# Chunked attention and a squared-ReLU feed-forward on one core: the next block's attention moves to the front of the input stage

## The chip, the cores and the metric

The kernel runs on one core of a Trainium2 chip. The metric is the device time of one execution in microseconds (us); before the change its median over 7 runs is 294.36 us (292.05 to 300.25). One execution was profiled. TensorE (PE; PEld is its weight load) does the matmuls, VectorE (DVE) and ScalarE (ACT) the element-wise work, GpSimd (POOL) casts and stores, and SyncE (SP) issues the loads and the transposing DMAs.

## The reference

Attention within chunks of 64 tokens, for 8 batches, 8 heads, 576 tokens and a head size of 64, and then a feed-forward network over the 4608 tokens, with 2048 inner features:

```python
scores = scale * np.matmul(q_c, k_c.transpose(0, 1, 2, 4, 3))   # q_c, k_c, v_c: (B, H, 9, 64, 64)
scores = scores - np.max(scores, axis=-1, keepdims=True)
attn = np.exp(scores)
attn = attn / (np.sum(attn, axis=-1, keepdims=True) + 1e-09)
out = np.matmul(attn, v_c)
x = out.transpose(0, 2, 1, 3).reshape(B * S, H * D)             # (4608, 512)
h = np.maximum(x @ w_in, 0.0)                                   # w_in (512, 2048)
return (h * h) @ w_out                                          # w_out (2048, 512)
```

Inputs and output are float32; the kernel multiplies in bfloat16 and accumulates in float32.

## The kernel before

**Groups and blocks.** The tokens are cut into 18 groups of 256, and two groups make a block of 512: blocks 0 to 8, where block 1 takes group 3 before group 2. A block has an input stage (`ffn_in`, x times w_in, ReLU and square) and an output stage (times w_out). While TensorE works on one block's feed-forward, the attention of the next block's groups (`nxt`) is put between its matmuls, and the loads, casts and transposes of the block after that (`far`) run on the other engines.

**Slots.** Nothing is scheduled by a planner: every instruction is issued in the order in which the Python code reaches it (`manual_schedule`), and each engine works through its own queue in order. The order of the work is set by slots. `ffn_in` and `ffn_out` are generators; each `yield` is a slot. After each slot the loop at L570 to L579 issues one load of the block's list (if the slot is in `go_slots`) and then whatever `at(slot, f, g)` has put into the plan. In blocks 2 to 8 the input stage has 16 slots (0 to 15), one per slice of 128 inner features, and the output stage 14 (16 to 29). Block 1 takes its two groups one after the other in its input stage, so it has 32 slots there and 14 in its output stage (32 to 45). Block 0 has 16 and 16.

**The steps of a group's attention**, by the short names used in the plan:

- `C` (L209): q and k are cast to bfloat16 (`qkb`), on POOL for groups below 8 and on ACT from there on.
- `TD` (L216): one transposing DMA, issued by SP, turns `qkb` into `qkT`. Groups 0 to 3 are transposed on TensorE instead (`TE`, `TA`, `TM`, L176), with two copies of q out of PSUM on DVE and two of k on ACT (L174).
- `SC` (L224): 32 small matmuls (L234) write the scores into a PSUM tile of the pool `ps_att`, which has two buffers; ACT takes the exponential (L241) into `e`.
- `AV` (L244): two sets of 32 small matmuls (L258), each into a `ps_att` tile, then for each set a reciprocal of the row sums (L265) and a multiplication (L266) on DVE, which give `x`.
- `XT` (L272): `x` becomes `xT`, the feed-forward's input. From group 6 on this is a transposing DMA issued by SP (L279); groups 2 to 5 are transposed on TensorE (L285), and one copy takes the result out of PSUM (L290), on ACT for group 2 and on DVE for the others.

**Feed-forward.** In a slot of `ffn_in` TensorE does four matmuls (L318) into one of four `ps_ffn` banks, ACT takes the ReLU (L329), and DVE the square (L333), or ACT for three slices of a block (L331). All of them need `xT` of the whole block, except in block 1, which takes 256 tokens at a time. The output stage of block 0 is plain (L464). That of the other blocks (`ffn_out`, L351) computes the two-by-two block product with seven products instead of eight: `product` (L386) runs two slots for each of them, into two PSUM chains "n" and "m", and between them DVE forms differences of the input (`d5`, `d2`, `d1`, `d6`, `d7`: one L346 instruction of 128x2048 each, into `w_st` tiles), adds the partial results (`nm`, `n1`, `o_sb`, L346 too) and ACT copies others. The sums of quarters of w_out that the products need (`sum_quarters`) are formed on DVE in blocks 0 and 1.

**SP's queue.** The loads of q, k and v, and the transposing DMAs TD and XT, stand in one queue on SP in the order of the slots. In block 2 the loads are v of groups 6 and 7 and then q, k and v of groups 8 and 9, one in each slot; XT of groups 6 and 7 and TD of groups 8 and 9 stand among them. Each of these DMAs also waits until the one eight places ahead of it has landed. The stores go out on POOL.

The functions that the change touches, and the code that calls them:

Of the kernel before, what the change touches and what calls it, by code (L numbers as in the profile page):

```python
# [17 lines left out]
def kernel(  # L18
# [9 lines left out]
    nc = tc.nc  # L28
# [243 lines left out]
    def transpose_x(g):  # L272
        j, c = place[g]
        if j not in xTs:
            xTs[j] = att_pool.tile([128, BT // 128, n_dt, 128], BF16, name="xT", bufs=2)
        x = state.pop(("x", g))
        dst = xTs[j][:, c // 128:c // 128 + 2].rearrange("p t h q -> p (t h) q")
        if g >= FIRST_DMA_X:
            nc.sync.dma_start_transpose(out=dst, in_=x.rearrange("p t h a d -> p (t h a d)"))  # L279
            return  # L280
        ps = ps_att.tile([128, 1024], FP32, name="ps_att")
        psb = ps.bitcast(BF16)[:, 0:1024].rearrange("p (b q) -> p b q", q=128)
        for t in range(2):
            for hp in range(n_hp):
                nc.tensor.transpose(  # L285
                    out=psb[:, t * n_hp + hp, :],
                    in_=x[:, t, hp].rearrange("p a d -> p (a d)"),
                    identity=ident)
        copy = nc.scalar.copy if g == 2 else nc.vector.tensor_copy
        copy(out=dst, in_=psb)  # L290

    C, TD = cast_qk, transpose_qk_dma
# [58 lines left out]
    def ffn_out(j):  # L351

        gT = gTs.pop(j)
        HT = BT // 2
        last = j == len(blocks) - 1
        a11, a12 = gT[:, 0:HF, 0:HT], gT[:, HF:, 0:HT]  # L360
        a21, a22 = gT[:, 0:HF, HT:], gT[:, HF:, HT:]

        def difference(x, y):
            d = wst_pool.tile([128, 1024], FP32, name="w_st").bitcast(BF16).rearrange(
                "p (a f) -> p a f", a=HF)
            add(nc.vector, d, x, y, ALU.subtract)
            return d

        n_tt = HT // 128
        banks = {}  # L370

        def chain(name):
            tiles = [ps_ffn.tile([128, 512], FP32, name="ps_ffn")
                     for _ in range(n_tt if last else 1)]
            banks[name] = [(tiles[t], 0, HD, t) for t in range(n_tt)] if last else [
                (tiles[0], 0, n_tt * HD, None)]
            return [tiles[t][:, 0:HD] if last else tiles[0][:, t * HD:(t + 1) * HD]
                    for t in range(n_tt)]

        def product(name, a, b, first):  # L380
            if first:
                state["chain", name] = chain(name)
            outs = state["chain", name]
            for t in range(n_tt):
                for i in range(HF):
                    nc.tensor.matmul(  # L386
                        out=outs[t],
                        lhsT=a[:, i, t * 128:(t + 1) * 128],
                        rhs=b[:, i, :],
                        start=(first and i == 0 and (last or t == 0)), stop=(i == HF - 1),  # L390
                        skip_group_check=True)
                yield

        def parts(name):
            for tile_, lo, n, t in banks[name]:
                at_ = (t or 0) * HD
                yield tile_[:, lo:lo + n], slice(at_, at_ + n), t

        def kept(name):
            return ffn_pool.tile([128, n_tt * HD], FP32, name=name)  # L400

        def store(dma, o_sb, half, col, t):
            t0 = blocks[j][half] * GT
            if t is None:
                dma.dma_start(  # L405
                    out=out[t0:t0 + HT, col:col + HD].rearrange("(t p) d -> p t d", p=128),
                    in_=o_sb.rearrange("p (t d) -> p t d", d=HD))
            else:
                dma.dma_start(
                    out=out[t0 + t * 128:t0 + (t + 1) * 128, col:col + HD],  # L410
                    in_=o_sb[:, t * HD:(t + 1) * HD])

        def o_tile():
            return ffn_pool.tile([128, n_tt * HD], FP32, name="o_sb", bufs=4)

        d5 = difference(a11, a12)
        d2 = difference(a22, a21)
        yield from product("n", a22, b11_p_b21, True)
        n1 = kept("n1")
        for ps, cols, t in parts("n"):  # L420
            nc.scalar.copy(out=n1[:, cols], in_=ps)
        yield from product("m", a11, b12_p_b22, True)
        w = kept("nm")
        for ps, cols, t in parts("m"):
            add(nc.vector, w[:, cols], ps, n1[:, cols])
        d1 = difference(a11, a22)
        yield from product("n", d5, b22, False)
        n2 = kept("n2")
        for ps, cols, t in parts("n"):
            nc.scalar.copy(out=n2[:, cols], in_=ps)  # L430
        d6 = difference(a21, a11)
        yield from product("m", d2, b11, False)
        c21 = o_tile()
        for ps, cols, t in parts("m"):
            add(nc.vector, c21[:, cols], w[:, cols], ps, ALU.subtract)
            store(nc.gpsimd, c21, 1, 0, t)
        d7 = difference(a12, a22)
        yield from product("n", d1, b11_m_b22, False)
        s = kept("n1")
        for ps, cols, t in parts("n"):  # L440
            add(nc.vector, s[:, cols], ps, n2[:, cols], ALU.subtract)
        c12 = o_tile()
        add(nc.vector, c12, w, n2, ALU.subtract)
        store(nc.gpsimd, c12, 0, HD, None)
        yield from product("m", d6, b11_p_b12, False)
        c22 = o_tile()
        for ps, cols, t in parts("m"):
            add(nc.vector, c22[:, cols], ps, s[:, cols])
            store(nc.gpsimd, c22, 1, HD, t)
        yield from product("n", d7, b21_p_b22, False)  # L450
        c11 = o_tile()
        for ps, cols, t in parts("n"):
            copy = nc.vector.tensor_copy if t else nc.scalar.copy
            copy(out=c11[:, cols], in_=ps)  # L454
            store(nc.gpsimd if t is None else nc.sync if t else nc.scalar, c11, 0, 0, t)
# [69 lines left out]
    for j, grps in enumerate(blocks):  # L525
# [4 lines left out]
        def at(slot, f, g):  # L530
            plan.setdefault(slot, []).append((f, g))

        if j == 0:
            loads, go_slots = pieces(far), range(17)
            at(28, sum_quarters(b11_p_b21, b11, b21), None)
            for slot, f in ((24, TA), (27, SC), (29, AV), (31, XT)):
                at(slot, f, nxt[0])
            at(31, TM, nxt[1])
            at(31, sum_quarters(b11_m_b22, b11, b22, ALU.subtract), None)
            phases = [ffn_in(0, [(0, 512, range(n_ft))]), ffn_out_by_ft(0)]  # L540
        elif j == 1:
            loads, go_slots = itertools.chain(*map(qk_pieces, far)), range(30, 48)
            for slot, f in ((3, SC), (6, AV), (11, XT)):
                at(slot, f, grps[1])
            for i, g in enumerate(nxt):
                for slot, f in ((16 + 4 * i, C), (21 + 4 * i, TD), (37, SC), (39 + 2 * i, AV),
                                (42 + 2 * i, XT)):
                    at(slot, f, g)
            for i, g in enumerate(far):
                at(36 + 4 * i, C, g)  # L550
                at(42 + 3 * i, TD, g)
            at(0, sum_quarters(b11_p_b12, b11, b12), None)
            at(12, sum_quarters(b12_p_b22, b12, b22), None)
            at(20, sum_quarters(b21_p_b22, b21, b22), None)
            phases = [ffn_in(1, [(0, 256, FT_ORDER), (256, 256, FT_ORDER)]), ffn_out(1)]
        else:
            loads, go_slots = pieces(far), range(32)
            slots = {SC: 8, AV: 11, XT: 15, C: 18, TD: 20}
            if j == 2:
                loads = itertools.chain(*map(v_pieces, nxt), loads)  # L560
                slots = {SC: 8, AV: 13, XT: 18, C: 22, TD: 24}
            for i, g in enumerate(nxt):
                at(slots[SC] + (3 if j == 2 else 2) * i, SC, g)
                at(slots[AV] + 3 * i, AV, g)
                at(slots[XT] + 3 * i, XT, g)
            for i, g in enumerate(far):
                at(slots[C] + 4 * i, C, g)
                at(slots[TD] + 4 * i, TD, g)
            phases = [ffn_in(j, [(0, BT, FT_ORDER)]), ffn_out(j)]
        slot = 0  # L570
        for phase in phases:
# [40 lines left out]
```

## Time and profile before

| | |
|---|---|
| median of 7 runs | 294.36 us |
| profiled execution | 294.64 us, its span 292.8 us |
| PE busy | 275.1 us (94%) |
| DVE, ACT, POOL busy | 191.1, 159.6, 55.0 us |
| mean granted TensorE clock | 0.988 |
| block 1's output stage begins | 67.1 us |
| blocks 2, 3, 4 begin (first L318) | 85.2, 117.3, 148.7 us |
| a later block (148.9 to 177.4) | 28.5 us |
| an L318 matmul, 128x512, mean | 364 ns |
| a difference (L346 w_st), mean | 1219 ns |
| x on DVE: L265 and L266, mean | 201 and 692 ns |
| exponential (L241), mean | 1019 ns |

"Busy" is the time in which an engine has an instruction at work; matmuls overlap in the pipeline, so their mean duration is longer than the distance between two of them. A row of the waits names the engine, line and tile that waited, then what it waited for, then the sum, the number and the longest of these waits. In the timeline a transposing DMA's time is that of its issue; when it lands is told by the view of the DMAs. A matmul of 512 columns follows the one before it after 0.213 us at the full clock.

### The profile page before, as it was taken

The page shows a single profiled execution, that of the slowest core. Times are in us where ns is not written, and L with a number is a line of the kernel's source. Part 1 is how long each engine was busy: PE and PEld are TensorE (multiplying, and loading weights), DVE is VectorE, ACT ScalarE, POOL GpSimd, SP SyncE. Part 2 cuts the span into 40 slices and gives each one's busy share as a digit, 9 for nine tenths or more (in the row PEclk, how much of TensorE's full clock was granted, in tenths as well). Part 3 has the DMA queues.
Part 4 walks back from the last instruction along what each step waited for, and adds up shares of the span by engine and source line. Part 5 has one row for each costly group of instructions (what it writes and reads, how often), then busy time and mean ns, then how long its engine had stood idle before and what let it go on. Part 6 is the DMA issues. An engine that isn't in the chain of part 4 may idle for free.

```text
span 292.8 us, 7284 instructions
## 1 busy us (share of the span) xinstructions
PE 275.1 (94%) x3011; PEld 179.5 (61%) x3014; DVE 191.1 (65%) x307; ACT 159.6 (55%) x268; POOL 55.0 (19%) x85
## 2 busy tenths in 40 slices
PE   2999999999889995999999999999999999999994
PEld 1764445888664585346854685468547844784583
DVE  1256514999563594168936994699469846974793
ACT  1527614983328652486558645963695378217710
POOL 2037734062071003000020002001100210020012
PEclk9999999999999999599999999999999999999999
DMA  7999999999998899999899969998997850311003
GB/s 201 239 337 359 361 311 231 283 208 205 200 211 235 189 203 238 254 196 199 194 299 221 169 149 286 213 147 170 296 214 127 106 183 2 74 73 72 2 16 127
DMA packets 156176, 57.09 MB, mean 195 GB/s; under 512 B 139312, under 2 KB 151856, under 8 KB 156144
## 3 DMA queue, kind: packets, MB, share of 16 engines
q1 hardware_dynamic: 153168, 47.33, 76.2%
q0 software_dynamic: 2832, 9.18, 8.8%
q8 instruction: 23, 0.38, 0.6%
q10 hardware_dynamic: 144, 0.13, 0.1%
q14 instruction: 9, 0.07, 0.1%
HBM read 36.70 MB, written 9.44 MB: 158 GB/s over the span
## 4 chain that ended last, share of the span: by engine, by line
PE 52%; DVE 6%; DMA 2%; issue 1%; ACT 1%; ACTq 0%
PE ps_ffn L318 28%; PE ps_ffn L386 21%; DVE x L266 2%; DVE w_st L346 2%; DMA xT<-x 2%; PE ps_att L234 1%; DVE gT L333 1%; ACT rl L329 1%; PE ps_att L258 1%; DVE rec L265 1%; DVE o_sb L454 0%; ACTq L329 0%
## 5 line engine op out<-in xcount | busy, mean ns | idle before, releaser
L318 PE MATMUL ps_ffn<-xT,w_in_bf 128*128 128x512 bf16 (+1 forms) x640 | 133.4, 364 | 3.3 <-DMA xT<-x 3.2
L333 DVE TENSOR_TENSOR gT<-rl 128x512 bf16<-128x512 f32 (+2 forms) x132 | 77.0, 604 | 65.2 <-ACT rl L329 62.5
L329 ACT ACTIVATE rl<-ps_ffn 128x512 f32<-128x512 f32 (+2 forms) x160 | 86.2, 553 | 33.2 <-PE ps_ffn L318 32.1
L318 PEld LDWEIGHTS <-w_in_bf 128*128 128x128 bf16 x640 | 61.0, 99 | 61.9 <-issue 7.7
L386 PEld LDWEIGHTS <-w_st 128*128 128x128 bf16 x640 | 61.9, 98 | 10.0 <-DVE w_st L346 1.9
L405 POOL DMA_DIRECT2D out_dram<-o_sb x29 | 20.7, 714 | 160.1 <-DVE o_sb L346 154.5
L346 DVE TENSOR_TENSOR w_st<-gT 128x2048 bf16<-128x2048 bf16 x40 | 47.4, 1219 | 0.2
L386 PE MATMUL ps_ffn<-w_out_bf,w_st 128*128 128x256 bf16 x384 | 45.1, 273 | 1.1 <-DVE nm L346 0.5
L386 PE MATMUL ps_ffn<-w_sum,w_st 128*128 128x256 bf16 x256 | 29.6, 273 | 0.1
L386 PEld LDWEIGHTS <-gT 128*128 128x128 bf16 x256 | 24.6, 98 | 5.1 <-DVE gT L333 0.8
L454 ACT COPY o_sb<-ps_ffn 128x512 f32<-128x512 f32 (+1 forms) x8 | 4.5, 558 | 41.5 <-PE ps_ffn L386 41.5
L266 DVE TENSOR_TENSOR x<-ps_att,rec 128x512 bf16<-128x512 f32 x36 | 24.9, 692 | 1.2
L241 ACT ACTIVATE e<-ps_att 128x1024 bf16<-128x1024 f32 x18 | 18.3, 1019 | 7.4 <-PE ps_att L234 7.3
L331 ACT ACTIVATE gT<-rl 128x512 bf16<-128x512 f32 (+2 forms) x28 | 16.8, 599 | 0.9
L386 PE MATMUL ps_ffn<-w_out_bf,gT 128*128 128x256 bf16 x128 | 15.6, 273 | 0.0
L386 PE MATMUL ps_ffn<-w_sum,gT 128*128 128x256 bf16 x128 | 15.5, 273 | 0.0
L464 PE MATMUL ps_ffn<-w_out_bf,gT 128*128 128x512 bf16 x61 | 14.3, 380 | 0.6 <-ACT rl L329 0.3
L430 ACT COPY n<-ps_ffn 128x512 f32<-128x512 f32 (+1 forms) x9 | 4.8, 537 | 14.3 <-PE ps_ffn L386 14.3
L140 POOL CAST w_in_bf<-w_st 128x1024 bf16<-128x1024 f32 (+1 forms) x9 | 8.8, 989 | 19.0 <-DMA w_st<-in_moe_w_in_dram 19.0
L265 DVE RECIPROCAL rec<-ps_att 128x8 f32<-128x8 f32 x36 | 7.2, 201 | 7.9 <-PE ps_att L258 7.9
L234 PEld LDWEIGHTS <-qkT 64*64 64x64 bf16 x576 | 6.3, 111 | 8.4 <-issue 5.7
L214 POOL CAST qkb<-q_sb 128x1024 bf16<-128x1024 f32 x4 | 6.9, 1728 | 23.1 <-DMA q_sb<-in_q_dram 23.1
(51 smaller groups left out, 168.6 us busy)
## 6 DMA issues: line engine op xcount, KB each, us to landing
out_dram<-o_sb POOLq DMA_DIRECT2D x33, 256.0 KB, 4.8
q_sb<-in_q_dram SPq DMA_DIRECT2D x25, 256.0 KB, 5.0
k_sb<-in_k_dram SPq DMA_DIRECT2D x25, 256.0 KB, 5.1
ve_sb<-in_v_dram SPq DMA_DIRECT2D x32, 128.0 KB, 4.6
vo_sb<-in_v_dram SPq DMA_DIRECT2D x32, 128.0 KB, 4.2
w_st<-in_moe_w_in_dram SPq DMA_DIRECT2D x8, 512.0 KB, 6.9
w_st<-in_moe_w_out_dram SPq DMA_DIRECT2D x8, 512.0 KB, 6.2
q_sb<-in_q_dram SPq DMA_DIRECT2D x3, 512.0 KB, 6.7
```

What stands on the lines that cost most here:

```text
L234: nc.tensor.matmul(out=ps[64 * c:64 * c + 64, o0:o0 + 64], lhsT=qkT[64 * a:64 * a + 64, 1, t, hp, cols], rhs=qkT[64 * a:64 * a + 64, 0, t, ...
L241: nc.scalar.activation(out=e.rearrange("p a h t q -> p (a h t q)"), in_=ps, func=AF.Exp, scale=scale)
L265: nc.vector.reciprocal(out=rec, in_=o[:, :, :, D])
L266: nc.vector.tensor_tensor(out=x[:, t].rearrange("p h a d -> p a h d"), in0=o[:, :, :, 0:D], in1=rec.to_broadcast([128, 2, n_hp, D]), op=AL ...
L318: nc.tensor.matmul(out=h[:, 0:n], lhsT=w_in_bf[:, dt, ft * 128:(ft + 1) * 128], rhs=xT[:, c // 128:(c + n) // 128, dt, :], start=(dt == 0) ...
L329: nc.scalar.activation(out=rl[:, 0:n], in_=h[:, 0:n], func=AF.Relu)
L331: nc.scalar.activation(out=gT[:, ft, c:c + n], in_=rl[:, 0:n], func=AF.Square)
L333: nc.vector.tensor_tensor(out=gT[:, ft, c:c + n], in0=rl[:, 0:n], in1=rl[:, 0:n], op=ALU.mult)
L346: engine.tensor_tensor(out=out, in0=in0, in1=in1, op=op)
L386: nc.tensor.matmul(out=outs[t], lhsT=a[:, i, t * 128:(t + 1) * 128], rhs=b[:, i, :], start=(first and i == 0 and (last or t == 0)), stop=( ...
L405: dma.dma_start(out=out[t0:t0 + HT, col:col + HD].rearrange("(t p) d -> p t d", p=128), in_=o_sb.rearrange("p (t d) -> p t d", d=HD))
L464: nc.tensor.matmul(out=o_ps[tt], lhsT=gT[:, ft, tt * 128:(tt + 1) * 128], rhs=w_out_bf[:, ft, :], start=(ft == 0), stop=(ft == n_ft - 1))
```

## The change

Five things are moved, and no arithmetic is changed:

1. Group 2's transposes on TensorE (`TM`) go from the last slot of block 0 to slot 1 of block 1; its scores follow in slot 4 instead of 3, its values in 7 instead of 6. The sum `b11_p_b12` goes from slot 0 to slot 2.
2. In block 1's output stage `SC` of the second group (5) goes one slot down, and `XT` of both groups (4 and 5) too; XT of group 5 is now in the block's last slot.
3. In block 1 the difference `d7` is formed before product "m" with d2 instead of after it, so that on DVE it stands ahead of the values of groups 4 and 5.
4. The copies of the transposed x of groups 4 and 5 run on ScalarE instead of DVE (group 3 stays on DVE, group 2 on ScalarE).
5. The plan of blocks 2 to 7 for the next block's groups: in block 2 `AV` goes from slots 13 and 16 to 12 and 14, and `XT` from 18 and 21 to 15 and 17. In blocks 3 to 7 `SC` goes from slots 8 and 10 to 2 and 5, `AV` from 11 and 14 to 6 and 9, `XT` from 15 and 18 to 10 and 13. The slots of `C` and `TD` stay.

```diff
-        copy = nc.scalar.copy if g == 2 else nc.vector.tensor_copy
+        copy = nc.vector.tensor_copy if g == 3 else nc.scalar.copy
         copy(out=dst, in_=psb)
...
         d6 = difference(a21, a11)
+        if j == 1:
+            d7 = difference(a12, a22)
         yield from product("m", d2, b11, False)
...
-        d7 = difference(a12, a22)
+        if j > 1:
+            d7 = difference(a12, a22)
         yield from product("n", d1, b11_m_b22, False)
...
-            at(31, TM, nxt[1])
             at(31, sum_quarters(b11_m_b22, b11, b22, ALU.subtract), None)
...
-            for slot, f in ((3, SC), (6, AV), (11, XT)):
+            for slot, f in ((1, TM), (4, SC), (7, AV), (11, XT)):
                 at(slot, f, grps[1])
             for i, g in enumerate(nxt):
-                for slot, f in ((16 + 4 * i, C), (21 + 4 * i, TD), (37, SC), (39 + 2 * i, AV),
-                                (42 + 2 * i, XT)):
+                for slot, f in ((16 + 4 * i, C), (21 + 4 * i, TD), (37 + i, SC), (39 + 2 * i, AV),
+                                (43 + 2 * i, XT)):
                     at(slot, f, g)
...
-            at(0, sum_quarters(b11_p_b12, b11, b12), None)
+            at(2, sum_quarters(b11_p_b12, b11, b12), None)
...
-            slots = {SC: 8, AV: 11, XT: 15, C: 18, TD: 20}
+            slots = {SC: (2, 5), AV: (6, 9), XT: (10, 13), C: (18, 22), TD: (20, 24)}
             if j == 2:
                 loads = itertools.chain(*map(v_pieces, nxt), loads)
-                slots = {SC: 8, AV: 13, XT: 18, C: 22, TD: 24}
-            for i, g in enumerate(nxt):
-                at(slots[SC] + (3 if j == 2 else 2) * i, SC, g)
-                at(slots[AV] + 3 * i, AV, g)
-                at(slots[XT] + 3 * i, XT, g)
-            for i, g in enumerate(far):
-                at(slots[C] + 4 * i, C, g)
-                at(slots[TD] + 4 * i, TD, g)
+                slots = {SC: (8, 11), AV: (12, 14), XT: (15, 17), C: (22, 26), TD: (24, 28)}
+            for f in (SC, AV, XT):
+                for i, g in enumerate(nxt):
+                    at(slots[f][i], f, g)
+            for f in (C, TD):
+                for i, g in enumerate(far):
+                    at(slots[f][i], f, g)
```

## The prediction

> **What bounds the kernel now.** I read the page's busy table and its forty slices first, to see which engine is full and where it isn't.
>
> ```profile
> PE 275.1 (94%) x3011; PEld 179.5 (61%) x3014; DVE 191.1 (65%) x307; ACT 159.6 (55%) x268; POOL 55.0 (19%) x85
> ...
> PEclk9999999999999999599999999999999999999999
> DMA  7999999999998899999899969998997850311003
> ```
>
> TensorE is busy for 94%, so an edit can pay only where TensorE stands still or runs slowly. One slice has half the clock (the seventeenth, 117 to 124 us). The DMA engines are full until 234 us, so a transfer can change places with another but not come for nothing. Then the waits of TensorE, and the one of the weight loads that recurs:
>
> ```profile
> PE ps_ffn L318 <- DMA xT<-x: 3.2, 1, 3.2
> PE ps_att L234 <- DMA qkT<-qkb: 1.4, 1, 1.4
> PE ps_att L285 <- DVE x L266: 0.9, 1, 0.9
> ...
> PE ps_ffn L386 <- DVE nm L346: 0.5, 1, 0.5
> ...
> PEld L386 <- DVE w_st L346: 1.9, 5, 0.4
> ```
>
> After start-up that is all there is to win: 3.2 us at the start of block 3 (xT of group 7), 1.4 and 0.9 in block 1's output stage, 0.5 in block 2's, and one short wait on the first difference, w_st, in each of blocks 3 to 7: there the spacing of two matmuls is 0.377 us in place of 0.109 (starts in the instruction record), so 0.27 us each. Then the start of block 3, by windows (stretch: length, PE busy, PEld, DVE, ACT, POOL, granted clock, DMA share, GB/s):
>
> ```profile
> 114.00:117.30 3.30, 0.07 (x1) 0.00 (x0) 0.00 (x0) 0.58 (x1) 0.78 (x2) 0.87 1.06 228
> 117.30:120.00 2.70, 2.70 (x7) 1.02 (x7) 0.11 (x1) 0.60 (x1) 0.00 (x0) 0.50 1.21 294
> 120.00:123.30 3.30, 3.30 (x10) 1.14 (x8) 1.28 (x2) 1.19 (x2) 0.00 (x0) 0.51 1.13 240
> 123.30:126.00 2.70, 2.70 (x14) 1.20 (x13) 1.33 (x2) 2.10 (x4) 0.00 (x0) 1.00 1.01 228
> ```
>
> The wait costs twice: 3.2 us of idleness, then 14 matmuls of 512 columns 0.427 us apart instead of 0.213, 3.0 us more. Last, SP's queue, which issues both the transposes that TensorE waits for and the loads (timeline, SP):
>
> ```profile
> 106.14 1.00 SPq L111 DMA_DIRECT2D k_sb<-in_k_dram  x1
> ...
> 107.19 1.36 SPq L118 DMA_DIRECT2D ve_sb<-in_v_dram  x2
> ...
> 108.71 1.55 SPq L279 DMA_TRANSPOSE xT<-x  x1
> ...
> 112.35 1.28 SPq L279 DMA_TRANSPOSE xT<-x  x1
> ...
> 116.18 3.64 SPq L220 DMA_TRANSPOSE qkT<-qkb  x1
> ...
> 120.54 2.21 SPq L220 DMA_TRANSPOSE qkT<-qkb  x1
> ```
>
> The DMA view has the time to landing: 3.8 us for the first xT, 4.9 for the second (117.26), and for the two qkT, which are groups 8 and 9 for block 3:
>
> ```profile
> qkT<-qkb SPq DMA_TRANSPOSE x1, 5.6
> ```
>
> So qkT of group 8 lands at 121.8 and that of group 9 (4.3 us) at 124.8. The casts for group 8 had ended at 108.9 us: what holds this transpose back is its place behind the loads, not its data. Block 3 starts at 117.3 and reads it at 128.1 (slot 8): 6.3 us to spare. This is the row on which the prediction turns.
>
> **The change part by part.**
>
> *Group 2's transposes (TM) from the end of block 0 to slot 1 of block 1.* The same 32 transposes, two DVE and two ACT copies; no DMA. In the old place TensorE works on them from 50.43 to 51.51 while DVE copies group 3's xT (50.54, 0.69 us). That cover goes: TensorE waits from 50.50 to about 51.3, +0.8 us. The copies keep three units of L318 (0.46 us each) ahead of SC(2), against the 1.1 us that ACT's pair takes: hidden. The sum b11_p_b12 (1.22 us on DVE) goes two units down: hidden behind L318, nothing reads it before block 1's output stage.
>
> *Block 1's output stage.* SC(5) one slot down: eight matmuls and SC(4) now stand before it, TensorE arrives after the 74.3 at which its qkT lands, -1.4. d7 (1.22 us) leaves the place between the two groups' values, and XT(4) goes one slot down: the wait for x goes, 0.95 idle, 1.22 in spacing. The x copies on ACT take 0.99 us (group 2's copy at 58.67) instead of 0.69 on DVE, and XT(5) is now in the last slot, so block 2's first L318 waits for that copy: +1.1. The m product of d6 may wait some 0.3 us for c21. Sum: 0.8 - 1.4 - 1.2 + 1.1 + (0 to 0.3): -0.7 to -0.4 us.
>
> *Block 2.* AV(6) and AV(7) go to slots 12 and 14. AV(6)'s second half needs the PSUM tile that exp(7) frees at 98.4, one unit after SC(7): some +0.7. In return DVE has done both x before the output stage, and w's add (nm) is in time: -0.54 idle, -0.8 in spacing. Block 2 ends at 113.5 to 114.1 instead of 114.07. Its XT each issue one DMA transpose: on SP they move from places 94 and 98 to 91 and 94. x(6) and x(7) are ready near 100.5 and 103, before SP comes to them, so nothing queued behind them waits longer. XT(6) goes out at 106.1; XT(7) behind it (1.55), the k load (1.0) and one ve load (0.76) at 109.4, landing with 3.8 to 4.9 at 113.2 to 114.3 instead of 117.26. The 3.2 us wait falls to 0 to 0.6, and block 3 starts at 114.1 (113.7 to 114.4).
>
> *Block 3, SC from slots 8 and 10 to 2 and 5.* Here the gain is given back. SC starts 2.73 us after the block's start for three units (slot 8 starts at 7.86, nine units). So TensorE comes to SC(8) at 116.8 and needs qkT(8). Its transpose stands at place 102 of SP's queue in both kernels, behind the same 101 transfers, with the engines full: it lands at 121.8 again. TensorE's queue is in order, so everything of block 3 from its fourth unit on stands behind it: a wait of 5.0 us, longer than the one removed. qkT(9) lands at 124.8 and is wanted at 125 or later: no second wait.
>
> The clock: the row says 3.0 us lost after 3.2 us of idleness. The Trainium skill ("TensorE: Matmul & The Clock Gate", Part 1) has one free-running window of about 3.4 us of work to win the clock back, which would be an estimated 1.7 us; here the half clock lasted from 116.4 to 123.2, 6.8 us, 5.9 of them at work. The same page ("Why this matters for your kernels") wants no gap over some 3 us, which speaks against this change: it lengthens the gap. I take the row, 3.0, with 1.7 to 3.4 (by where the window falls) for the range.
>
> End of block 3: a whole block takes 28.52 (148.91 to 177.43 in the chain). Less the 2.73 done and the 0.27 of the wait on w_st, which goes because DVE's x work (two times 0.89 us) has left the end of the input stage, 25.5 are left. 121.9 + 25.5 + 3.0 = 150.4, against 148.91: +1.5 (+0.2 to +1.9 by the clock, and 1 for each us that the landing moves).
>
> *Blocks 4 to 7.* SC, AV and XT in front: the same instructions. Their second qkT lands 2.8, 1.3, 1.2 and 3.0 us after the block's start (151.5, 178.6, 207.0, 237.4) and is wanted 5.8 us after it: hidden. ACT has two exps (1.02) and two squares (0.63) in the first seven units; by its rows exp of the second group ends about 0.1 us after AV wants its tile, as now. What is won is the wait on w_st, 4 x 0.27 = 1.1. The xT transposes land still earlier than now, which is worth nothing. Bounds: 0 to -1.3.
>
> *Sum.* What blocks 0 to 2 win or lose vanishes in the wait for qkT(8), as long as it is under 5 us. +1.5 - 1.1 = +0.4 on the span of 292.8. The profiled execution took 294.64, 0.3 above the median of 294.36; with the same difference the median becomes 294.8.
>
> **The rivals.**
>
> *A, the wait changes its name* (the forecast): 0.62. 293 to 297, most of it within 0.5%, which is 1.5 us and about what a measurement here can tell from no change.
>
> *B, qkT(8) comes in time.* If moving xT up, or another course of the queue, lets it land before 117, the 3.2 and the 3.0 go, and five times 0.27: -7.5, 287 us. Landing at 119 the wait is 2.2, perhaps too short for the clock to fall: 289. For it: the transpose's data is there ten us before. Against: equal places in the queue, and 1.06 to 1.21 of DMA share in just this stretch. 0.16, at 287 to 291.
>
> *C, slower: the second qkT of blocks 4 to 7 is late too.* Two xT transposes now stand before the v loads in each block, and qkT behind those. It decides from 2.8 us of delay on (5.8 less 3.0, block 7; block 4 the next at 3.0). Each us beyond is one for each block concerned, and a wait of 2 us or more brings up to 3 of half clock. Two blocks with 1 to 2 us: 297 to 299. Against: in these blocks the qkT transposes wait for ACT's casts (172.96, 201.48, 230.01), so SP has caught up there. With A's own upper end beyond 297 by a later landing: 0.22.
>
> Faster by over 0.5%: B and 0.06 of A, 0.22. Within: 0.36. Slower: 0.20 of A and C, 0.42. The range cuts off a tenth at each end: 289.5 to 298.5; A's own is 293 to 297.
>
> **What would show it.** Right: at block 3 no wait on xT over 0.6 us, and one at L234 on qkT of about 5 us with the half clock after it; no waits on w_st; a wait of about 1 us on the xT copy at the starts of blocks 1 and 2; none on qkT in blocks 4 to 7. Wrong: qkT(8) landing before 119 (B), or waits at L234 after 150 us (C).

## The result and the profile after

The changed kernel takes 296.62 us (median of 23 runs, 294.89 to 298.86); the kernel before, 294.68 in the runs beside it. The ratio is 1.0093, with a 95% interval of 1.0072 to 1.0115: slower by 0.9%. The ratios here compare the executions within 1.5% of the fastest of their kernel, while the medians are of all executions, so the two can differ (by these medians it is 0.7%). The profiled execution took 295.54 us with a span of 293.8, 1.0 more than before.

TensorE's granted clock in the page of the changed kernel, by fortieths of the span, and the DMA engines' share:

```profile
PEclk9999999999999999689999999999999999999999
DMA  7999999998998899999999979999989951111003
```

The stretch at half clock is still there, now in the seventeenth and eighteenth slices. The waits of TensorE after start-up (engine, line and tile that waited, what it waited for, sum, number, longest):

```profile
PE ps_att L234 <- DMA qkT<-qkb: 5.9, 1, 5.9
...
PE ps_ffn L318 <- ACT xT L290: 1.1, 1, 1.1
PE ps_att L258 <- ACT e L241: 0.8, 2, 0.7
PE ps_ffn L318 <- DVE xT L290: 0.8, 1, 0.8
...
PE ps_att L285 <- DVE x L266: 0.3, 1, 0.3
```

The wait on xT (3.2 us) is gone, so are those on x and qkT in block 1's output stage and on nm in block 2 (the 0.3 us on x shown here is another one, of group 2), and no weight load waits for w_st any more. In their place stands one wait of 5.9 us on qkT. The windows around it (length, busy time of PE, PEld, DVE, ACT, POOL, granted clock, DMA share, GB/s):

```profile
114.00:117.50 3.50, 3.50 (x24) 2.11 (x22) 0.90 (x2) 1.54 (x3) 1.66 (x3) 1.00 0.81 221
117.50:123.70 6.20, 0.41 (x2) 0.00 (x0) 0.79 (x2) 1.47 (x3) 0.00 (x0) 0.70 1.09 227
123.70:128.30 4.60, 4.52 (x44) 1.89 (x44) 0.86 (x2) 2.22 (x3) 0.00 (x0) 0.66 1.05 226
128.30:132.00 3.70, 3.70 (x78) 1.90 (x78) 2.97 (x7) 3.23 (x5) 0.00 (x0) 1.00 0.96 207
```

TensorE does three units of block 3 and stops at 117.9 until 123.8. The clock is at half from 120.0 to 126.8, so of these 6.8 us only 3.1 are spent at work, and its matmuls lose half of that, 1.5 us. And SP's queue in the same stretch (timeline):

```profile
106.44 2.39 SPq L279 DMA_TRANSPOSE xT<-x  x1
...
110.17 1.74 SPq L279 DMA_TRANSPOSE xT<-x  x1
...
116.51 5.17 SPq L220 DMA_TRANSPOSE qkT<-qkb  x1
...
122.40 2.18 SPq L220 DMA_TRANSPOSE qkT<-qkb  x1
```

```profile
qkT<-qkb SPq DMA_TRANSPOSE x1, 7.2
```

The second xT goes out at 110.2 instead of 112.4, but qkT of group 8, qkT(8) for short, at 116.5, as before (116.2), though its casts had ended at 110.8. It took 7.2 us to land (the DMA view of this issue), at 123.7; qkT(9) landed at 128.3. The starts of the blocks, taken from the first L318 of each:

| us | block 2 | 3 | 4 | 5 | 6 | 7 | 8 | end |
|---|---|---|---|---|---|---|---|---|
| before | 85.2 | 117.3 | 148.7 | 177.3 | 205.8 | 234.3 | 262.8 | 292.8 |
| after | 85.9 | 115.2 | 150.8 | 179.0 | 207.3 | 235.5 | 263.7 | 293.8 |

Block 3 takes 35.6 us instead of 31.4; a later block 28.25 instead of 28.52.

### The profile page after: what moved, and what is told of

The parts are those of the page before. It is cut to its first block, busy times and chain, and to the rows that moved or that the text cites. A ratio compares the mean times of both kernels' runs of the same rounds, so it can differ in the third digit from the quotient of the medians.

```text
span 293.8 us, 7277 instructions
## 1 busy us (share of the span) xinstructions
PE 273.2 (93%) x3011; PEld 180.4 (61%) x3014; DVE 190.5 (65%) x305; ACT 162.0 (55%) x270; POOL 55.1 (19%) x85
## 4 chain that ended last, share of the span: by engine, by line
PE 78%; ACT 6%; DMA 5%; SPq 5%; issue 3%; DVE 2%; POOL 0%; ACTq 0%
PE ps_ffn L318 35%; PE ps_ffn L386 34%; PE ps_ffn L467 4%; ACT rl L329 4%; DMA w_st<-in_moe_w_in_dram 3%; DMA qkT<-qkb 2%; PE ps_att L258 2%; ACT e L241 2%; SPq L118 1%; SPq L103 1%; SPq L125 1%; PE ps_att L234 1%; DVE x L266 1%; SPq L137 1%; PE ps_att L285 1%
## 5 line engine op out<-in xcount | busy, mean ns | idle before, releaser
L318 PE MATMUL ps_ffn<-xT,w_in_bf 128*128 128x512 bf16 (+1 forms) x640 | 132.2, 361 | 2.3 <-ACT xT L290 1.1
L333 DVE TENSOR_TENSOR gT<-rl 128x512 bf16<-128x512 f32 (+2 forms) x132 | 75.9, 597 | 66.4 <-ACT rl L329 65.1
L318 PEld LDWEIGHTS <-w_in_bf 128*128 128x128 bf16 x640 | 60.4, 98 | 59.5 <-issue 3.0
L405 POOL DMA_DIRECT2D out_dram<-o_sb x29 | 20.7, 714 | 159.7 <-DVE o_sb L346 154.2
L234 PE MATMUL ps_att<-qkT 64*64 64x64 bf16 x576 | 8.8, 201 | 6.3 <-DMA qkT<-qkb 5.9
L258 PEld LDWEIGHTS <-e 64*64 64x64 bf16 x576 | 7.2, 107 | 8.8 <-issue 3.8
```

The lines of the kernel that those rows point to most:

```text
L234: nc.tensor.matmul(out=ps[64 * c:64 * c + 64, o0:o0 + 64], lhsT=qkT[64 * a:64 * a + 64, 1, t, hp, cols], rhs=qkT[64 * a:64 * a + 64, 0, t, ...
L258: nc.tensor.matmul(out=ps[64 * p:64 * p + 64, a, hp * (D + 1):(hp + 1) * (D + 1)], lhsT=e[64 * c:64 * c + 64, a, hp, t, :], rhs=vb[64 * c: ...
L318: nc.tensor.matmul(out=h[:, 0:n], lhsT=w_in_bf[:, dt, ft * 128:(ft + 1) * 128], rhs=xT[:, c // 128:(c + n) // 128, dt, :], start=(dt == 0) ...
L333: nc.vector.tensor_tensor(out=gT[:, ft, c:c + n], in0=rl[:, 0:n], in1=rl[:, 0:n], op=ALU.mult)
L405: dma.dma_start(out=out[t0:t0 + HT, col:col + HD].rearrange("(t p) d -> p t d", p=128), in_=o_sb.rearrange("p (t d) -> p t d", d=HD))
```

## The experiments

The theory, Q: the transposed tiles of block 3 land when the stream of DMAs lets them; the change makes TensorE want qkT of groups 8 and 9 earlier than that, and pays there. Rivals: K, the uncovered x copies and the moved transposes of blocks 0 and 1 cost the time; F, attention in front crowds ACT and PSUM in all blocks 3 to 7. Ratios are to the kernel before, measured beside each run.

**Which part holds the loss.** e1 takes block 3's slots back:

```diff
+            if j == 3:
+                slots = {SC: (8, 10), AV: (11, 14), XT: (15, 18), C: (18, 22), TD: (20, 24)}
```

> The changed kernel with block 3's attention back in its old slots (SC 8 and 10, AV 11 and 14, XT 15 and 18); all else stays. Theory Q (the queue: block 3's pace is set by when qkT of groups 8 and 9 land, 123.7 and 128.3 us in the changed kernel's trace, whatever TensorE does): TensorE comes to SC(8) about 7.9 us after the block's start at 115.2, waits 0 to 1 us there, reaches SC(9) near 126 and waits up to 2.3 us for 128.3; then five units of 0.855 us more are already done than in the changed kernel: 4.3 us faster than it, 0.985 to 0.995 of the kernel before. Rival K (the uncovered x copies of block 1 and TM's move cost the time): no faster than the changed kernel, 1.005 to 1.01. Rival F (attention in front crowds ACT and PSUM in all blocks 3 to 7): a fifth of the loss comes back, about 1.007.

Measured: 294.59 us, ratio to the kernel before 0.9957 (0.9904 to 1.0009). The loss is gone, as Q has it, though 0.9957 lies just outside the range that Q gave; with the wide interval no gain over the kernel before is shown. In its profile the wait has moved on: 2.7 us on xT at block 4.

f3 moves block 3's attention alone to the front, in the kernel before; all else stays as it was:

```diff
-            slots = {SC: 8, AV: 11, XT: 15, C: 18, TD: 20}
+            slots = {SC: (8, 10), AV: (11, 14), XT: (15, 18), C: (18, 22), TD: (20, 24)}
...
+            if j == 3:
+                slots = {SC: (2, 5), AV: (6, 9), XT: (10, 13), C: (18, 22), TD: (20, 24)}
```

> The kernel before with block 3's attention alone in front (SC 2 and 5, AV 6 and 9, XT 10 and 13). Theory Q: after the wait on xT block 3 meets SC(8) at 120 to 122 and SC(9) at about 124 to 126, while their qkT land at 121.8 to 125 and 125 to 128.3: one or two waits more, 1 to 3 us, longer at half clock: 1.003 to 1.012, all of the changed kernel's loss or more. If the loss is in the other parts: 0.998 to 1.002, for the wait on xT already covers that on qkT.

Measured: 297.40 us, 1.0117 (1.006 to 1.0174), from six executions: as much as the whole loss, from moving one block's attention. Its waits and windows (views as above):

```profile
PE ps_att L234 <- DMA qkT<-qkb: 6.6, 2, 6.0
...
PE ps_ffn L318 <- DMA xT<-x: 0.8, 1, 0.8
```

```profile
119.60:125.60 6.00, 0.05 (x2) 0.00 (x2) 0.60 (x1) 1.23 (x2) 0.00 (x0) 0.73 1.25 173
125.60:130.00 4.40, 4.40 (x43) 1.98 (x44) 0.69 (x1) 2.03 (x3) 0.00 (x0) 0.59 0.94 209
```

The same 6 us of standing still and the same half clock. Here the wait on xT was 0.8 us and not the 3.2 of the kernel before's profile, so it covered little.

**Blocks 0 and 1.** e2 undoes parts 1 to 4 of the change:

```diff
-        copy = nc.vector.tensor_copy if g == 3 else nc.scalar.copy
+        copy = nc.scalar.copy if g == 2 else nc.vector.tensor_copy
...
-        if j == 1:
-            d7 = difference(a12, a22)
...
+            at(31, TM, nxt[1])
...
-            for slot, f in ((1, TM), (4, SC), (7, AV), (11, XT)):
+            for slot, f in ((3, SC), (6, AV), (11, XT)):
...
-                for slot, f in ((16 + 4 * i, C), (21 + 4 * i, TD), (37 + i, SC), (39 + 2 * i, AV),
-                                (43 + 2 * i, XT)):
+                for slot, f in ((16 + 4 * i, C), (21 + 4 * i, TD), (37, SC), (39 + 2 * i, AV),
+                                (42 + 2 * i, XT)):
...
-            at(2, sum_quarters(b11_p_b12, b11, b12), None)
+            at(0, sum_quarters(b11_p_b12, b11, b12), None)
```

> The changed kernel with its parts 1 to 4 undone (TM, the sum, SC, XT, d7 and the copies of blocks 0 and 1 as before); blocks 2 to 7 stay changed. Theory Q: what blocks 0 and 1 win or lose ends in the wait for qkT(8), which lands when it lands: 1.005 to 1.012, within 0.3% of the changed kernel. Rival K (the waits of 0.8 and 1.1 us on the x copies are the loss): about 1.9 us faster than the changed kernel, 1.001 to 1.004. The opposite (parts 1 to 4 win time): slower than the changed kernel by 0.3% or more.

Measured: 295.35 us, 1.0043 (1.0018 to 1.0069). That is faster than the changed kernel by 0.5%, outside what Q had said and just above K's range; its profile still has 5.4 us of wait on qkT at block 3. It is also less than f3's 1.0117, though it has f3's move in it; the intervals overlap, so what block 3 costs by itself is known only roughly, 0.6 to 1.7%. g2, below, comes back to blocks 0 and 1.

**The place in the queue.** e3 moves no work of TensorE; it changes the order of transfers in block 2, and for that takes the two groups' casts on ScalarE four slots up:

```diff
-                slots = {SC: (8, 11), AV: (12, 14), XT: (15, 17), C: (22, 26), TD: (24, 28)}
+                slots = {SC: (8, 11), AV: (12, 14), XT: (15, 17), C: (18, 22), TD: (19, 23)}
+                go_slots = [*range(17), *range(24, 32)]
```

> The changed kernel with the transposes of q and k for groups 8 and 9 moved up in SP's queue of block 2 (C in slots 18 and 22, TD in 19 and 23) and the ten loads of v for these groups, which stood before them, put behind them. The same transfers, another order. Theory Q: qkT(8) lands near 116, qkT(9) near 119, before TensorE wants them (118 and 121), the wait at SC(8) falls from 5.9 to under 1 us and the clock holds; values wait up to 1 us for v: 6 to 8 us faster than the changed kernel, 0.978 to 0.99 of the kernel before. If the transposes themselves are slow when the queue is full, not their place: under 2 us, 1.003 or more. Rivals K and F: no more than 0.3% from the changed kernel.

Measured: 294.10 us, 0.9977 (0.9932 to 1.0021): 1.1% faster than the changed kernel, half of what Q expected. Its waits:

```profile
PE ps_att L234 <- DMA qkT<-qkb: 2.0, 3, 1.2
PE ps_ffn L318 <- ACT xT L290: 1.1, 1, 1.1
PE ps_att L258 <- DMA vo_sb<-in_v_dram: 1.0, 1, 1.0
```

Its SP queue, and the landing of the first of the two qkT (DMA view):

```profile
110.92 6.41 SPq L220 DMA_TRANSPOSE qkT<-qkb  x2
117.38 1.76 SPq L118 DMA_DIRECT2D ve_sb<-in_v_dram  x2
...
qkT<-qkb SPq DMA_TRANSPOSE x1, 5.4
```

qkT(8) and qkT(9) landed at 116.3 and 121.5 instead of 123.7 and 128.3. In the changed kernel the casts of group 8 had ended 5.7 us before its transpose went out, so there it was the place and not the data. Block 3 ended at 146.9 instead of 150.8. But two of the three waits on qkT are block 4's (0.4 and 1.2 us): there the next pair came 7.2 and 8.5 us after its issue, at 149.9 and 154.2, later than in the changed kernel (148.3 and 151.7); block 3's four stores went out in just that time (142.8 to 148.6). So Q was too narrow: by these landings the stream stays behind through block 4. That the stores hold it up was not tried apart.

**The half clock.** e4 fills the wait with work that is not used:

```diff
+                    if j == 3 and f is SC and i == 0:
+                        at(slots[f][i], keep_busy, 70)
                     at(slots[f][i], f, g)
```

> The changed kernel with 70 matmuls of the identity (128 columns, some 4.7 us) put before SC(8) in block 3, which fill most of the wait so that the clock does not fall; their result is not used. As the prediction's sum has it (wait and half clock add up): 1.7 to 3.4 us faster than the changed kernel, near 1.0. Theory Q with the second landing (TensorE came to SC(9) at 128.3, just when qkT(9) landed): at the full clock it comes there at about 127 and waits for 128.3, so the half clock cost nothing: within 0.3% of the changed kernel. If the 70 outlast the wait: slower by the rest.

Measured: 295.49 us, 1.0056 (1.0019 to 1.0093). The profiled execution has the clock at 1.00 throughout after start-up and this wait in front of SC(8), the scores of group 8:

```profile
PE ps_att L234 <- DMA qkT<-qkb: 1.6, 1, 1.6
```

It ended at 123.6, as in the changed kernel, and block 4 began at 149.2 instead of 150.8. These 1.5 us in the profile are what the changed kernel's matmuls lost at half clock. The gain by the ratios, 0.4% or about 1.1 us, lies between the two expectations, and the intervals overlap. f5 does the same to the wait on xT in the kernel before:

```diff
+            if j == 2:
+                at(29, keep_busy, 40)
             phases = [ffn_in(j, [(0, BT, FT_ORDER)]), ffn_out(j)]
```

> The kernel before with 40 matmuls of the identity (some 2.7 us) in the last slot of block 2, which stand where TensorE waits for xT before block 3; their result is not used. It prices the half clock in the kernel before. If the profiled execution (6.8 us of half clock, 3.0 us lost) is the rule: 2 to 3 us faster, 0.990 to 0.993. If its clock loss was above the mean (the mean granted clock of its runs, 0.995, is 3 us of half clock, 1.5 lost): 0.994 to 1.0. If the matmuls stand in the way (the wait is often shorter than they are): above 1.0.

Measured: 295.29 us, 1.0003 (0.9966 to 1.0041). No gain is shown, though the runs' mean granted clock rose from 0.995 to 0.997. An estimate from that rise, 0.002 x 293 us, puts only 0.6 us at stake, less than the interval can tell. In the profile block 4 now waits 0.7 us for xT; that the stream takes back what TensorE wins here fits this and isn't shown by it.

**The gains that were to be.** f1 is block 2's part alone on the kernel before, whose other slots stay:

```diff
-                slots = {SC: 8, AV: 13, XT: 18, C: 22, TD: 24}
+                slots = {SC: (8, 11), AV: (12, 14), XT: (15, 17), C: (22, 26), TD: (24, 28)}
```

> The kernel before with block 2's new slots alone (AV 12 and 14, XT 15 and 17). Theory Q (transposed tiles land when the DMA stream lets them, and TensorE can only choose where it waits): the 3.2 us wait on xT at block 3 falls under 1 us; of the 3 to 6 us won, waits of up to 2.5 us at SC(8) and SC(9) in slots 8 and 10 and one of up to 2.7 us on xT at block 4 (as in e1) take half back: 0.985 to 1.0. If the wait on xT is all that stands there: 0.975 to 0.982. If the new slots in block 2 lose (exp for AV(6) late by 0.7 us): above 1.0.

f2 is the part of blocks 4 to 7 alone:

```diff
-            slots = {SC: 8, AV: 11, XT: 15, C: 18, TD: 20}
+            slots = {SC: (2, 5), AV: (6, 9), XT: (10, 13), C: (18, 22), TD: (20, 24)}
...
+            if j == 3:
+                slots = {SC: (8, 10), AV: (11, 14), XT: (15, 18), C: (18, 22), TD: (20, 24)}
```

> The kernel before with the attention of blocks 4 to 7 alone in front (SC 2 and 5, AV 6 and 9, XT 10 and 13). The prediction's term: the wait on w_st goes in four blocks, 4 x 0.27 = 1.1 us: 0.996 (0.993 to 0.9985). Rival C (the second qkT of these blocks comes too late for slot 5) or rival F (ACT and PSUM crowded): above 1.0.

f1: 294.51 us, 1.0002 (0.996 to 1.0043), no gain. The wait at block 3 is gone, and in its place stands this one, at block 4 (f1's waits):

```profile
PE ps_ffn L318 <- DMA xT<-x: 2.7, 1, 2.7
```

f2: 293.67 us, 1.0028 (0.9995 to 1.0061). Its blocks 5 to 7 take 28.25 us in the trace instead of 28.52, so the 0.27 us each are real, and F falls: attention in front makes these blocks shorter, not longer. Whether the whole gains by it is open: the ratio leaves room for 0.15 us, but the medians of all executions, 293.67 against 294.52, differ by 0.85 us the other way.

**A version from the theory.** f4 keeps e3's order of transfers, and has TensorE want each qkT when it is there:

```diff
+            slots = {SC: (7, 9), AV: (10, 12), XT: (14, 16), C: (18, 22), TD: (20, 24)}
...
+            if j == 3:
+                slots = {SC: (4, 7), AV: (9, 12), XT: (13, 15), C: (18, 22), TD: (20, 24)}
```

> A version made from theory Q: blocks 0 and 1 as before; block 2 as in e3 (its new slots, and qkT of groups 8 and 9 ahead of v of these groups in the queue); block 3 with SC 4 and 7, AV 9 and 12, XT 13 and 15; blocks 4 to 7 with SC 7 and 9, AV 10 and 12, XT 14 and 16, late enough for their qkT and early enough for DVE to be free at the end of the input stage. Theory Q: no wait of TensorE over 1 us after block 2 and no half clock: 5 to 7 us faster than the kernel before, 0.976 to 0.985. If the stream as a whole is behind, so that each order only moves the wait: 0.99 to 1.0.

Measured: 293.03 us, 0.9955 (0.9921 to 0.9988). That is faster than the kernel before but far from Q's 0.976 to 0.985; it is the range foretold for a stream that is behind as a whole. Its profiled execution (one of its longer ones) has no half clock after start-up and no wait at block 3, but one of 2.0 us on qkT in block 4 and 0.5 us for DVE in each of blocks 4 to 7. g1 corrects both, with the change's parts 1 to 4:

```diff
-            slots = {SC: (7, 9), AV: (10, 12), XT: (14, 16), C: (18, 22), TD: (20, 24)}
+            slots = {SC: (7, 9), AV: (10, 13), XT: (14, 16), C: (18, 22), TD: (20, 24)}
...
+            if j == 4:
+                slots = {SC: (9, 11), AV: (12, 14), XT: (15, 17), C: (18, 22), TD: (20, 24)}
```

> The changed kernel's parts 1 to 4 with a plan made from f4's trace: block 2 and the queue as in e3 and f4, block 3 as in f4 (SC 4 and 7, AV 9 and 12, XT 13 and 15), block 4 later (SC 9 and 11, AV 12 and 14, XT 15 and 17) for f4's wait of 2.0 us on qkT there, blocks 5 to 7 with SC 7 and 9, AV 10 and 13, XT 14 and 16, for the 0.5 us that AV waited for DVE in each block. Theory Q: what parts 1 to 4 win early is given back to the stream, the waits named go: 1 to 3 us faster than f4, 0.985 to 0.992 of the kernel before. If the stream only moves the wait on to block 5: as f4, 0.993 to 0.998.

Measured: 291.89 us, 0.9902 (0.9868 to 0.9935), as Q had it: 1% faster than the kernel before and nearly 2% than the changed one. The profiled execution is the fastest of the 22; its page and its longest waits after start-up:

```profile
PEclk9999999999999999999999999999999999999999
```

```profile
PE ps_att L258 <- ACT e L241: 1.5, 3, 0.7
PE ps_ffn L318 <- ACT xT L290: 1.1, 1, 1.1
PE ps_ffn L318 <- DVE xT L290: 0.8, 1, 0.8
...
PE ps_att L258 <- DVE x L266: 0.7, 2, 0.5
```

After start-up TensorE waits for v alone among the DMAs, 0.2 us. Block 3 runs from 114.5 to 142.6 and the span is 287.2. g2 is g1 with parts 1 to 4 undone, by e2's diff:

> g1 with parts 1 to 4 undone (blocks 0 and 1 as in the kernel before). e2 left open whether these parts cost time where a wait on the stream follows them. Here no long wait follows, so their own price shows: by the two traces they trade the waits on qkT (about 1 us, up to 1.7) and x (0.95) in block 1's output stage for those on the two x copies (0.79 and 1.10). Theory Q: within 0.4% of g1, 0.986 to 0.994 of the kernel before. Rival K (parts 1 to 4 cost 1.5 us or more): 0.985 or less. If they win: 0.994 or more.

Measured: 291.69 us, 0.9935 (0.9898 to 0.9972), beside g1's 0.9902: where no long wait follows, parts 1 to 4 do not cost the 1.5 us of their own that K needs. The traces speak for a small gain instead. In all seven experiments with the old place of group 2's transposes (TM), TensorE waits 0.7 to 1.9 us there for k of group 2; the profile of the kernel before, from which they were priced, has no such wait (timelines of the kernel before and of f2):

```profile
50.94 0.64 PE L165 MATMUL ps_ffn<-ident,k_sb 128*64 128x128 bf16 x16
...
52.28 0.64 PE L165 MATMUL ps_ffn<-ident,k_sb 128*64 128x128 bf16 x16 [1.03 <-DMA k_sb<-in_k_dram]
```

In the new place no wait for k is left. Why e2 was all the same faster than the changed kernel stays open, and with it what parts 1 to 4 do where the long wait on qkT follows them; a shift of block 1's stores against the stream is possible and wasn't tried.

## Why the prediction was right or wrong

The forecast was 294.8 us and no clear change, with 0.42 for slower; measured were 296.62 and 0.9% slower, inside the range of 289.5 to 298.5. The course was as told: the wait on xT goes, one on qkT(8) takes its place, because that transpose kept its place in the queue, and block 3 gives back more than was won. f3 and e3 show this. That what the first blocks win or lose vanishes in this wait, e2 does not bear out: without parts 1 to 4 it was 0.5% faster. The sizes were not all right, and two of the errors offset each other.

- *Copies uncovered in block 1.* Said +0.8 and +1.1; the waits are 0.79 and 1.10. AV(6) waits 0.66 for exp, said 0.7; AV(7) waits another 0.2. Block 2 starts at 85.9, not at 84.7: 0.7 us of that had been lost by the end of block 0, before any changed instruction.
- *The wait on xT.* Said 0 to 0.6, measured none, in part by luck: xT landed at 114.95, said 113.2 to 114.3, but block 3 also started at 115.2. At the 114.1 that was said, it would have waited 0.8.
- *qkT(8).* The position in the queue was right (issue at 116.5). Its landing at 121.8 was carried over from the one profile, and that was the earliest: in the eight other traces with this order of transfers it landed at 123.2 to 125.6. So the wait was 5.9 and not 5.0 us.
- *qkT(9).* "Wanted at 125 or later: no second wait" came true for a reason that the sum missed: TensorE arrived at 128.3, held up by the half clock, just as it landed. At full clock it would have waited 1.4 us. So in this execution wait and half clock partly cover each other; in e4 qkT(9) landed at 125.4, and filling the wait saved the 1.5 us.
- *The clock, and the terms that were mis-sized.* "Block 3: +1.5" came from 121.9 + 25.5 + 3.0 = 150.4. The sum has the right terms. With the measured end of the wait, and half of the time at work under half clock, it gives the start of block 4 in four traces:

  | us | wait on qkT(8) ends | at work at half clock | sum: end + 25.5 + half of it | block 4 starts |
  |---|---|---|---|---|
  | said | 121.9 | 5.9 | 150.4 | |
  | changed kernel | 123.8 | 3.1 | 150.8 | 150.8 |
  | e2 | 125.0 | 4.0 | 152.6 | 152.5 |
  | f3 | 125.6 | 3.6 | 152.9 | 152.8 |
  | e4 | 123.6 | 0 | 149.1 | 149.2 |

  So for the changed kernel the sum had the landing 1.9 us too early and the clock 1.5 us too dear. That block 4 began within 0.4 us of what was said is luck.
- *The base.* The +1.5 was counted from one execution, in which block 3 lost 3.0 us to the clock. Its mean granted clock was 0.988, where 63 runs of that kernel have a mean of 0.995. f2 is the same kernel up to block 4; in its trace block 3 had no half clock, and block 4 began at 147.0 instead of 148.7. It paid later, with a wait of 2.1 us on xT and a half clock of 3.4 at block 4, and began block 5 at 177.0, against 177.3. So where the kernel before pays differs between executions, and a credit for its half clock in block 3 can't be read from one. f3, against many executions of the kernel before, puts block 3's move at 1.2%, about 3.4 us (1.8 to 5.1), where the sum said 1.5.
- *From the profile to the median.* Between the two profiles the span grew by 1.0 us, of which 0.4 was foretold. The medians differ by 1.9, since the changed kernel's profile is 1.1 us faster than its median. Three of its five longest executions had a granted clock of 0.983 instead of the profile's 0.988; none of them was traced, so what they waited for is not on record.
- *Clock rule against row.* The row said 3.0 us lost. The Trainium skill ("TensorE: Matmul & The Clock Gate", Part 1) has at least one window of about 3.4 us of work to win the clock back; for one window that is an estimated 1.7 us lost. The changed kernel lost 1.5, f3 1.8, e2 2.0: here the skill's window was the better guide. The half clock itself lasted 6.83 us in all three, but part of it passed while TensorE stood still. That the window runs freely fits the traces: in each of them the time from one change of the clock to the next is a multiple of 3.413 us.
- *Blocks 4 to 7.* Said -1.1: from the start of block 4 the profile gains 1.1 us (143.0 instead of 144.1). Whether the median keeps it, f2 leaves open.
- *Rivals.* B (qkT in time) needed another order of transfers, which e3 made; its price of -7.5 us was too high, since the next tiles were late then. C didn't happen in the changed kernel: no wait on qkT after block 3.

## What to carry to other kernels

In this kernel, with TensorE 94% busy and the DMA engines full, moving a consumer forward moved the wait to the next tile unless its transfer also moved. Before putting work earlier, list for each operand when it lands and when it is wanted, and spend only the difference. Here 6.3 us to spare at slot 8 were to pay for six slots (5.1 us) and for the 3.2 us of wait and 3.0 us of half clock that were to go. And take a landing and a stall from several executions: the 6.3 us rested on the earliest landing of nine. When a stall lowers the clock, count only the time at work under the lower clock.

## What the runs showed of the hardware

A transposing DMA of the same shape took 3.6 us from issue to landing at best (block 6 of the kernel before) and 7 to 9 us where stores went out beside it (e3, block 4), and its issue held SP's queue for 1.6 to 5.7 us (the longest in f4). Between start-up and the end, the half clock came in stretches of 3.41 or 6.83 us, and not always during the wait: in f1 TensorE was idle until 147.5 us, and the clock fell at 148.8, when it was working again, for 3.4 us. The length of the wait alone did not decide it: the clock fell with waits of 1.96 us (g2) and 2.09 us (f2), and in e3 after waits of 0.45 and 1.0 us, close together; it did not fall with 2.04 us (f4) or 1.6 us (e4).
